# One attention weight in four transfers of 128 rows, in place of one with four rows per partition

## The chip, the core and the metric

The kernel runs on one core of one Trainium2 chip. A core has a matrix engine (PE, with its weight loads shown as PEld), a vector engine (DVE), a scalar engine (ACT), GpSimd (POOL), and a sequencer that here issues nearly all transfers (SP). Sixteen DMA engines move data between the chip's main memory and the core's on-chip memory, which has 128 partitions. The metric is the device time of one execution in microseconds (us); the time of a kernel is the median of its runs.

## What is computed

One token of a decoder block in bfloat16: a layer norm without gain, attention of 32 query heads over a cache of 8 key/value heads with 65,536 positions of 128 numbers each, and a gated layer behind it, both with a residual.

```python
def _A_ref(x, k_cache, v_cache, wq, wo):            # x: 1 x 1 x 512, wq: 512 x 4096
    q = (x @ wq).reshape(B, Sq, Hq, Dh) ...
    scores = jnp.einsum("bhqd,bhkd->bhqk", q, k) * (Dh ** -0.5)
    p = _softmax(scores, axis=-1)
    o = jnp.einsum("bhqk,bhkd->bhqd", p, v)
    return o... @ wo
h = x + _A_ref(_layernorm(x, axis=-1), A_k_cache, A_v_cache, A_wq, A_wo)
h2 = h + _B_ref(_layernorm(h, axis=-1), B_w_gate, B_w_up, B_w_down)   # sigmoid(g) * u, then w_down
```

The caches K and V are 134 MB each. Beside them the weights are small: `wq` and `wo` have 4 MB each, the three weights of the gated layer 5.5 MB together.

## The kernel before

**A list of operations.** The class `Prog` collects, for each engine, a list of operations in the order in which that engine is to run them. Each has names that it waits for (`deps`) and may have a name itself; `emit` turns the names into semaphore waits. A transfer (`dma`) has a semaphore of its own group. An engine works strictly in the order of its list, so a wait holds up everything behind it on that engine. SP's list is nothing but transfers. The first transfer of SP and the first of ACT are taken out of the lists and put ahead of the start-up barrier of the program (lines 192 to 210), so they are issued at once; all others follow behind that barrier.

**The order of the transfers on SP** (lines 341 to 374): first `wq` (line 341, into the buffer `ktw`); then the K cache of head 0 in four transfers of 4 MB, which wait for nothing (lines 343 to 346, issued by line 339 in `load`); then for heads 1 to 7 K and V in halves of 8 MB, alternately (lines 347 to 351), each waiting until the part of the ring buffer that it overwrites has been read; then the last V, `wo` in two parts, the last V's second half, and the weights of the gated layer (`wg`, `wu`, and `wd` in four parts of 8, 3, 2 and 1 rows per partition, 128 partitions each). All of these go through one queue (q1). ACT issues one transfer, the vector `x` of 1 KB (line 325, queue q10).

**`wq` and `x` at the start.** One transfer brings `wq` as 512 rows of 4096 numbers (8 KB a row); partition p receives rows 4p to 4p+3 one behind the other. The vector x must stand in the same order: `x_col[p, k]` is x[4p + k]. It arrives as 16 rows of 32 (`xs`), is spread over the partitions by a matmul with a selecting matrix (line 423), masked and summed by DVE (lines 424 and 427), and goes through the layer norm: sums on DVE (`ln_stats`, lines 400 and 401), totals by a matmul with ones (line 403), mean and variance on DVE (lines 408 to 412), the power -1/2 on POOL (line 414). Line 432 writes the normed x into `xz`, from `hT` (which holds x in the order of `x_col`), the mean and `rstd`.

**The projection** (`project_q`, line 466, called by the operation in line 485) is 32 matmuls: for each of 8 groups of 512 columns four, one for each of the four rows that a partition holds. The operation waits for `wq` and `xz` before its first matmul. It is listed under line 443, where all matmuls with register addresses are made. ACT copies the result out (line 486), DVE transposes it (line 489), ACT spreads it (line 491) and writes the first head's weights (line 500).

**The main part.** For each block of keys DVE transposes chunks of K from the ring into `ktw` (line 531); `ktw` is the buffer that held `wq`, so the first transpose waits for the end of the projection (line 526). PE multiplies the transposed chunks with q (line 443). When DVE has transposed a set of chunks, a tiny DVE operation (line 534) marks it, and SP issues the transfer that overwrites them. Softmax (lines 562 to 580), the transposition of the probabilities (line 587) and the products with V (line 443 again, `ring,PT_sb`) follow for each head.

**The end** is the gated layer: matmuls with `wg` and `wu` (line 847), the gate (lines 854 to 863), matmuls with `wd` (line 866), the copy of the result (lines 884 and 885) and its store (line 886).

Of the kernel before, what the change touches and what calls it, by code (L numbers as in the profile page):

```python
# [10 lines left out]
ALU = mybir.AluOpType  # L11
# [4 lines left out]
NQ = 32  # L16
DH = 128
# [7 lines left out]
NKT = 8  # L25
# [10 lines left out]
class Prog:  # L36
# [14 lines left out]
    def op(self, eng, fn, deps=(), name=None, to=None, times=1):  # L51
        assert name is None or name not in self.where, name
        self.ops[eng].append(dict(fn=fn, deps=[d for d in deps if d], name=name, dma=None, to=to, times=times, part=self.part.get(eng)))
        if name:
            self.where[name] = (eng, len(self.ops[eng]) - 1)

    def dma(self, eng, fn, sem, deps=(), name=None):
        self.op(eng, fn, deps, name)
        rec = self.dma_sems.setdefault(sem, dict(sem=None, count=0))
        rec["count"] += 16  # L60
        self.ops[eng][-1]["dma"] = (sem, rec["count"])
# [162 lines left out]
def bass_sequential_preLN__gqa_block_cached__glu_gated_glu__decode_kernel(  # L224
# [10 lines left out]
    CH = TC * DH  # L235
# [11 lines left out]
    with ExitStack() as es:  # L247
        def sb(name, shape, dt):
            return es.enter_context(nc.sbuf_tensor(name, shape, dt))

        gsel = sb("gsel", [128, 128], fp32)
        hz = sb("hz", [128, 128], fp32)
        identf = sb("identf", [128, 128], fp32)
        onesf = sb("onesf", [128, 128], fp32)
        lsel = sb("lsel", [128, 128], fp32)
        iota_i = sb("iota_i", [128, 128], i32)
        ident = sb("ident", [128, 128], bf16)
# [7 lines left out]
        ktw = sb("ktw", [128, NKT * CH + WH], bf16)  # L265
# [9 lines left out]
        XR = 16  # L275
        xs = sb("xs", [XR, D // XR], bf16)
# [4 lines left out]
        xz = sb("xz", [128, 4 * 16], bf16)  # L281
        qh = sb("qh", [32, 512], bf16)
        qt = sb("qt", [32, 512], bf16)
        hT = [sb(f"hT{i}", [128, 4], fp32) for i in range(2)]
        sq = sb("sq", [128, 4], fp32)
        st = [sb(f"st{i}", [128, 2], fp32) for i in range(2)]
        mo = [sb(f"mo{i}", [128, 4], fp32) for i in range(2)]
        rstd = [sb(f"rstd{i}", [128, 1], fp32) for i in range(2)]
# [26 lines left out]
        def ps(bank, c0, c1, p0=0, p1=128):  # L315
            return PS[p0:p1, bank * 512 + c0: bank * 512 + c1]
# [5 lines left out]
        op, dma = P.op, P.dma  # L322
# [10 lines left out]
        def load(k, h, q, deps, sem, name, cols=None):  # L333
# [4 lines left out]
            at = (first_chunk(k, h, q) - j0) * CH  # L338
            dma("sp", lambda e: e.dma_start(ring[:, at + a * CH:at + z * CH], rows[:, (a - j0) * CH:(z - j0) * CH]), sem, deps, name)  # L339

        dma("sp", lambda e: e.dma_start(ktw[:, 0:NKT * CH].rearrange("p (k n) -> p k n", k=4),
                                        A_wq.rearrange("(p k) n -> p k n", p=128)), "r0", (), "wq")
        for q in range(2):
            for i in range(2):
                j0 = 16 * q + 8 * i
# [52 lines left out]
        def ln_stats(i, parts, dep, bank, c0):  # L398

            op("dve", lambda e: e.tensor_tensor_reduce(hT[i][:, :], parts[0], parts[1], 1.0, 0.0, ALU.add, ALU.add, st[i][:, 0:1]), [dep], f"hT.{i}")  # L400
            op("dve", lambda e: e.tensor_tensor_reduce(sq[:, :], hT[i][:, :], hT[i][:, :], 1.0, 0.0, ALU.mult, ALU.add, st[i][:, 1:2]),
               [f"hT.{i}"], f"st.{i}")
            op("pe", lambda e: e.matmul(ps(bank, c0, c0 + 2), lhsT=onesf[:, :], rhs=st[i][:, :], start=True, stop=True),
               [f"st.{i}", "onesf"], f"tot.{i}")

        def ln_rstd(i, bank, c0, factor):

            op("dve", lambda e: e.tensor_scalar(mo[i][:, 0:2], ps(bank, c0, c0 + 2), 1.0 / D, None, op0=ALU.mult),
               [f"tot.{i}"], f"mo.{i}")
            op("dve", lambda e: e.tensor_tensor(mo[i][:, 2:3], mo[i][:, 0:1], mo[i][:, 0:1], ALU.mult), [f"mo.{i}"], f"m2.{i}")  # L410
            op("dve", lambda e: e.tensor_tensor(mo[i][:, 3:4], mo[i][:, 1:2], mo[i][:, 2:3], ALU.subtract), [f"m2.{i}"], f"var.{i}")
            op("dve", lambda e: e.tensor_scalar(ve[i][:, :], mo[i][:, 3:4], eps, factor, op0=ALU.add, op1=ALU.mult),
               [f"var.{i}"], f"ve.{i}")
            op("pool", lambda e: e.tensor_tensor(rstd[i][:, :], ve[i][:, :], nhalf[:, :], ALU.pow), [f"ve.{i}", "nhalf"],
               f"rstd.{i}")


        n = 128 // XR
# [9 lines left out]
        op("dve", lambda e: None, ["zf"])  # L428
        ln_stats(0, (x_col[:, :], bass.AP(tensor=zf, offset=0, ap=[[1, 128], [0, 4]])), "xcol", 0, 0)
        ln_rstd(0, 0, 0, 1.0)  # L430
        xz_dst = bass.AP(tensor=xz, offset=8, ap=[[4 * 16, 128], [16, 4]])
        op("dve", lambda e: e.tensor_scalar(xz_dst, hT[0][:, :], mo[0][:, 0:1], rstd[0][:, 0:1], op0=ALU.subtract,
                                            op1=ALU.mult), ["rstd.0", "xz0"], "xz")
        def addr_of(t, elements=0):
            return nc.lookup_mloc(t).addr + 2 * elements

# [45 lines left out]

        op("act", lambda e: e.activation(ps(1, 0, 512, 0, 8), bass.AP(tensor=zcol, offset=0, ap=[[1, 8], [0, 512]]), AF.Copy), ["zcol"], "zq")
        op("act", lambda e: e.activation(ps(5, 0, 512), bass.AP(tensor=zcol, offset=0, ap=[[1, 128], [0, 512]]), AF.Copy), (), "zy")
        op("pe", project_q, ["zq", "zy", "xz", "wq", "identf", "lsel", "onef", "sel", "gsel", "row", "PTz", "qz0"], "q")
        op("act", lambda e: e.activation(  # L486
            bass.AP(tensor=qh, offset=0, ap=[[512, 8], [64, 8], [32, 2], [1, 32]]), psap(1, 0, [[64, 8], [1, 2], [2, 32]], 0, 8), AF.Copy),
           ["q", "qh0"], "qh")
# [307 lines left out]
        for i in range(HKV + 1):  # L796
            loop, last = 0 < i < HKV, i == HKV
            for r in range(NR):
# [26 lines left out]
                if not last and r == 3:  # L825
# [9 lines left out]
                                                   op0=ALU.mult, op1=ALU.add), ["tot.1"], "hc")  # L835
# [6 lines left out]
        for i, (nm, bank) in enumerate((("wg", GB), ("wu", UB))):  # L842
            at = W_AT[nm]
            for kt in range(4):
                for c in range(4):
# [3 lines left out]
                        rhs=ring[:, at + kt * FF + c * FG: at + kt * FF + (c + 1) * FG],  # L849
                        start=(kt == 0), stop=(kt == 3), tile_position=(0, 32 * c)),  # L850
# [66 lines left out]
```

## Time and profile before

| | |
|---|---|
| time, median of 3 runs | 656.33 us (656.27 to 656.4) |
| span of the profiled execution | 655.0 us |
| time above that span | 1.33 us (656.33 - 655.0) |
| mean granted clock of PE | 0.786 |
| busy: PE, DVE, ACT, POOL | 397.5, 350.3, 43.1, 3.7 us |
| moved by the DMA engines | 282.33 MB |

The span goes from the first to the last instruction of one profiled execution. For that execution the record holds the span and not a device time; the difference between the median of the runs and the span, 1.33 us, is taken as what lies around the span, and is the same in all the arithmetic below.

How to read it: the profile's page gives busy time by engine, the span in 40 slices, the DMA queues, the chain of work that ended last, the costliest groups of instructions, and the transfers with their time from issue to landing. In the views by window, each row gives a stretch of the span, the busy time of each engine with the number of its instructions, then PE's granted clock, the busy share of the DMA engines, and the rate in GB/s (packets are counted where they start, so in a short stretch the share can be over 1).

### The profile page before, as it was taken

What the parts mean: (1) busy time and instruction counts of PE and PEld (TensorE: products, weight loads), DVE (VectorE), ACT (ScalarE), POOL (GpSimd) and SP (SyncE); (2) the same over time, 40 slices, a digit from 0 to 9 for tenths busy, and PEclk for the clock granted to TensorE, in tenths of its full rate; (3) what the DMA queues carried; (4) which work ended last, traced back from release to release, by engine and by line L of the source; (5) the groups of instructions that cost most, each with busy time, mean ns of one, the idle gap of its engine ahead of it and who ended that gap; (6) DMA issues with size and microseconds to landing.
All of it is one profiled execution on the core that took longest, in us unless ns stands there. A gap on an engine that the chain in (4) does not pass through costs nothing.

```text
span 655.0 us, 6176 instructions
## 1 busy us (share of the span) xinstructions
PE 397.5 (61%) x2317; PEld 66.7 (10%) x1549; DVE 350.3 (53%) x428; ACT 43.1 (7%) x114; POOL 3.7 (1%) x19
## 2 busy tenths in 40 slices
PE   2778672937548293674828467392845739285466
PEld 1100010110101000010100101010010101001122
DVE  3398853819266290935719184481917548092202
ACT  1100200020000200002000200002000020001101
POOL 1000000000000000000000000000000000000000
PEclk9799695977959687785968769596796958878656
DMA  9999999999999999999999999999999989999998
GB/s 400 432 434 462 424 408 448 448 448 412 420 448 448 432 400 448 448 448 404 428 448 448 436 396 448 448 448 416 416 448 448 448 384 448 448 448 424 417 412 363
DMA packets 6372, 282.33 MB, mean 431 GB/s; under 512 B 738, under 2 KB 868, under 8 KB 1252
## 3 DMA queue, kind: packets, MB, share of 16 engines
q1 hardware_dynamic: 6340, 282.33, 99.7%
q10 hardware_dynamic: 32, 0.00, 0.0%
HBM read 282.33 MB, written 0.00 MB: 431 GB/s over the span
## 4 chain that ended last, share of the span: by engine, by line
DMA 66%; DVE 30%; PE 2%; issue 1%; SPq 0%; PEldq 0%
DMA ring<-in_A_k_cache_dram 58%; DVE ktw L531 30%; DMA ring<-in_B_w_up_dram 4%; DMA ring<-in_A_v_cache_dram 4%; PE PS L443 2%; PE PS L866 0%; PE PS L847 0%; DVE hh L859 0%; DVE hhT L863 0%; SPq L368 0%; SPq L339 0%; DVE y_sb L884 0%; PEldq L171 0%
## 5 line engine op out<-in xcount | busy, mean ns | idle before, releaser
L531 DVE STREAM_TRANSPOSE ktw<-ring 128x1024 f32<-128x1024 f32 x256 | 291.5, 1208 | 165.0 <-DMA ring<-in_A_k_cache_dram 165.0
L443 PE MATMUL PS<-ktw 128*128 128x512 bf16 x1024 | 276.3, 419 | 163.4 <-DVE ktw L531 155.8
L443 PE MATMUL PS<-ring,PT_sb 128*32 x1024 | 85.0, 420 | 55.0 <-issue 46.6
L443 PEld LDWEIGHTS PS<-ktw 128*128 x256 | 26.2, 102 | 401.5 <-issue 234.3
L618 ACT ACTIVATE po_sb<-PS,rl 128x512 bf16<-128x512 f32 x8 | 5.5, 687 | 523.4 <-PE PS L443 523.4
L443 PEld LDWEIGHTS PS<-ring,PT_sb 128*32 x1024 | 20.7, 116 | 117.5 <-issue 116.2
L566 DVE TENSOR_REDUCE gmj<-PS 1x4 f32<-1x128 f32 x8 | 2.2, 278 | 53.5 <-PE PS L564 53.5
L538 DVE TENSOR_REDUCE M_sb<-PS 128x1 f32<-128x512 f32 x32 | 19.9, 683 | 19.3 <-PE PS L443 19.3
L577 ACT ACTIVATE P_sb<-PS,negmax 128x512 bf16<-128x512 f32 x32 | 21.6, 686 | 0.3
L587 DVE STREAM_TRANSPOSE PT_sb<-P_sb 128x512 bf16<-128x512 bf16 x32 | 19.9, 674 | 1.7 <-ACT P_sb L577 1.7
L443 PE MATMUL PS<-ktw,xz 128*8 x32 | 9.6, 476 | 6.1 <-DMA ktw<-in_A_wq_dram 6.1
L634 DVE TENSOR_TENSOR Lw<-O,blk_of 128x896 bf16<-128x896 bf16 (+1 forms) x2 | 1.4, 682 | 15.9 <-ACT O L624 15.9
L489 DVE STREAM_TRANSPOSE qt<-qh 32x512 bf16<-32x512 bf16 x1 | 0.7, 699 | 14.8 <-ACT qh L486 14.8
L571 PE MATMUL PS<-one_f,gmrep 1*128 1x1 f32 x16 | 4.7, 358 | 5.0 <-DVE gmrep L568 5.0
L564 PE MATMUL PS<-identf,gm 128*1 128x128 f32 x16 | 4.5, 380 | 5.1 <-issue 2.9
L643 DVE CAST O<-PS 128x28 bf16<-128x28 f32 (+1 forms) x2 | 0.3, 174 | 12.8 <-PE PS L640 12.8
L577 ACT ACTIVATION_READ_ACCUMULATOR P_sb<-PS,negmax 128x1 f32 x32 | 6.5, 203 | 0.0
L621 PE MATMUL PS<-sel_bf,po_sb 128*128 128x4 bf16 x32 | 2.1, 170 | 6.3 <-ACT po_sb L618 6.3
L504 ACT ACTIVATE PS<-zcol 128x512 f32<-128x512 bf16 x8 | 5.0, 622 | 0.0
L573 ACT ACTIVATE negmax<-PS 128x1 f32<-128x1 f32 x8 | 1.4, 171 | 54.0 <-PE PS L571 54.0
L571 PEld LDWEIGHTS PS<-one_f,gmrep 1*128 1x128 f32 x16 | 4.0, 307 | 8.8 <-DVE gmrep L568 8.8
L592 PE MATMUL PS<-L_sb,lsel 128*128 128x4 f32 x16 | 2.5, 229 | 3.8 <-DVE PT_sb L587 3.8
(90 smaller groups left out, 65.4 us busy)
## 6 DMA issues: line engine op xcount, KB each, us to landing
ring<-in_A_k_cache_dram SPq DMA_DIRECT2D x4, 4096.0 KB, 34.8
ring<-in_A_v_cache_dram SPq DMA_DIRECT2D x1, 5120.0 KB, 30.1
ktw<-in_A_wq_dram SPq DMA_DIRECT2D x1, 4096.0 KB, 12.2
ktw<-in_A_wo_dram SPq DMA_DIRECT2D x1, 3584.0 KB, 18.4
ring<-in_A_v_cache_dram SPq DMA_DIRECT2D x1, 3072.0 KB, 36.9
ring<-in_B_w_gate_dram SPq DMA_DIRECT2D x1, 1792.0 KB, 23.4
ring<-in_B_w_up_dram SPq DMA_DIRECT2D x1, 1792.0 KB, 27.2
ring<-in_B_w_down_dram SPq DMA_DIRECT2D x1, 1024.0 KB, 29.2
```

Of the source, the lines that this page charges most:

```text
L443: return e.add_instruction(mybir.InstMatmult(name=nc.get_next_instruction_name(), engine=mybir.EngineType.PE, ins=[rhs, lhsT], outs=[e.low ...
L504: op("act", lambda e: e.activation(ps(PO, 0, 512), bass.AP(tensor=zcol, offset=0, ap=[[1, 128], [0, 512]]), AF.Copy), ["zcol"] if h == 0 e ...
L531: op("dve", lambda e, d=dst, sr=src: e.transpose(d, sr), deps, f"T{b}.{c}", to="T")
L538: op("dve", lambda e, u=u: e.tensor_reduce(M_sb[:, u % 4:u % 4 + 1], ps(u % NS, 0, 512), AX.X, ALU.max), [f"S{b}.{NC - NR + k}"], f"mx{u}" ...
L564: op("pe", lambda e: e.matmul(ps(MISC, 0, 128, 0, 1), lhsT=gm[:, :], rhs=identf[:, :], start=True, stop=True), [f"gm{h}"], f"gmT{h}", to="Q")
L566: op("dve", lambda e: e.tensor_reduce(gmj[:, :], ps(MISC, 0, 128, 0, 1).rearrange("p (i a c) -> p a i c", a=4, c=NC), AX.XY, ALU.max), [f" ...
L571: op("pe", lambda e: e.matmul(ps(MISC, 128, 129), lhsT=gmrep[0:1, :], rhs=one_f[0:1, 0:1], start=True, stop=True), [f"gmrep{h}"], f"neg{h}")
L577: op("act", lambda e, b=b: e.activation(P_sb[:, (b % 4) * 512:(b % 4 + 1) * 512], ps(b % NS, 0, 512), AF.Exp, bias=negmax[:, k:k + 1], sca ...
L587: op("dve", lambda e, b=b: e.transpose(PT_sb[:, (b % 4) * 512:(b % 4 + 1) * 512], P_sb[:, (b % 4) * 512:(b % 4 + 1) * 512]), [f"E{b}"], f" ...
L592: op("pe", lambda e: e.matmul(ps(MISC, 132, 136), lhsT=lsel[:, :], rhs=L_sb[:, :], start=True, stop=True), [f"PT{NR * h + NR - 1}"], f"l{h ...
L618: op("act", lambda e: e.activation(po_sb[:, :], ps(PO, 0, 512), AF.Copy, scale=rl[:, :]), [f"PV{h}.{NR - 1}", f"rl{h}"], f"po{h}", to="po")
L621: op("pe", lambda e, t=t: e.matmul(ps(OX, 0, 4), lhsT=po_sb[:, t * 128:(t + 1) * 128], rhs=sel_bf[:, 8 * t:8 * t + 8:2], start=(t == 0), s ...
```

## The change

`wq` comes in four transfers. Transfer k brings rows 128k to 128k+127, one row of 8 KB to each partition, into the k-th quarter of the same place. Partition p then holds rows p, 128+p, 256+p and 384+p. Only the first of the four is the first transfer of SP and so stands ahead of the start-up barrier. Each has a semaphore of its own, and the projection waits for all four.

x has to stand in the new order for the projection: `xz` now takes x[128k + p]. Four small matmuls bring the 16 rows of `xs` into this order in a bank of PE's result memory (bank 7, columns 48 to 52), each for 32 partitions; they pick columns of the identity matrix with a step of 4. The layer norm's sums go on as they were, from `x_col` in the old order, and so does the residual.

```diff
-        dma("sp", lambda e: e.dma_start(ktw[:, 0:NKT * CH].rearrange("p (k n) -> p k n", k=4),
-                                        A_wq.rearrange("(p k) n -> p k n", p=128)), "r0", (), "wq")
+        for k in range(4):
+            dma("sp", lambda e, k=k: e.dma_start(ktw[:, k * NQ * DH:(k + 1) * NQ * DH], A_wq[128 * k:128 * k + 128, :]), f"q{k}", (), f"wq{k}")
...
+        for j in range(4):
+            op("pe", lambda e, j=j: e.matmul(ps(7, 48, 52, 32 * j, 32 * j + 32), lhsT=xs[:, :], rhs=ident[0:XR, j:XR:4], start=True, stop=True,
+                                             tile_position=(0, 32 * j)), ["x", "ident"] if j == 0 else (), "xq" if j == 3 else None)
         xz_dst = bass.AP(tensor=xz, offset=8, ap=[[4 * 16, 128], [16, 4]])
-        op("dve", lambda e: e.tensor_scalar(xz_dst, hT[0][:, :], mo[0][:, 0:1], rstd[0][:, 0:1], op0=ALU.subtract,
-                                            op1=ALU.mult), ["rstd.0", "xz0"], "xz")
+        op("dve", lambda e: e.tensor_scalar(xz_dst, ps(7, 48, 52), mo[0][:, 0:1], rstd[0][:, 0:1], op0=ALU.subtract,
+                                            op1=ALU.mult), ["rstd.0", "xz0", "xq"], "xz")
...
-        op("pe", project_q, ["zq", "zy", "xz", "wq", "identf", "lsel", "onef", "sel", "gsel", "row", "PTz", "qz0"], "q")
+        op("pe", project_q, ["zq", "zy", "xz", "wq0", "wq1", "wq2", "wq3", "identf", "lsel", "onef", "sel", "gsel", "row", "PTz", "qz0"], "q")
```

## The prediction

> **What bounds the kernel now.** I read the page first: the 40 slices, the queues, and the chain of work that ended last.
>
> ```profile
> span 655.0 us, 6176 instructions
> ...
> DMA  9999999999999999999999999999999989999998
> ...
> DMA packets 6372, 282.33 MB, mean 431 GB/s; under 512 B 738, under 2 KB 868, under 8 KB 1252
> ...
> q1 hardware_dynamic: 6340, 282.33, 99.7%
> ...
> DMA 66%; DVE 30%; PE 2%; issue 1%; SPq 0%; PEldq 0%
> ```
>
> The DMA engines are busy in every slice, the queue q1 for 99.7% of the span. The chain gives DVE 30%, but that alone doesn't say that DVE holds up a transfer. So I looked at the rate in stretches of 19.3 us, at the beginning, and at the long middle.
>
> ```profile
> 0.00:1.00 1.00, 0.00 (x0) 0.00 (x0) 0.00 (x0) 0.00 (x0) 0.20 (x4) 1.00 0.00 0
> 1.00:2.75 1.75, 0.00 (x0) 0.00 (x0) 1.39 (x5) 1.68 (x2) 1.73 (x11) 1.00 1.13 318
> ...
> 11.40:30.70 19.30, 13.43 (x41) 3.71 (x36) 5.20 (x5) 3.24 (x7) 0.00 (x0) 0.85 1.00 433
> 30.70:50.00 19.30, 14.91 (x61) 1.44 (x15) 18.35 (x18) 0.00 (x0) 0.00 (x0) 0.97 1.01 436
> ...
> 69.30:599.40 530.10, 322.27 (x1840) 48.61 (x1168) 295.72 (x335) 31.43 (x88) 0.00 (x0) 0.78 1.00 435
> ```
>
> The last column is GB/s. From 11.4 us on it is 433 to 436, and 435 over 530 us. The stream of transfers begins at 1.0 us, loses something in its first 1.75 us, and then has one rate to the end. 8 MB (8.389 MB, one half of a head's K or V) take 8.389 / 435 = 19.3 us. Now the chain in order of time, for one round of DVE and transfer:
>
> ```profile
> 84.16 24.75 DMA ring<-in_A_k_cache_dram
> 108.91 0.02 issue
> 108.93 13.67 DVE ktw L531 x13
> ```
>
> This K half is issued at 84.16 and lands 24.75 us later. 19.3 of these are its own bytes; 5.4 are left. The first transfer of the kernel, ahead of which nothing stands in the queue, shows how long a lone transfer's lag is:
>
> ```profile
> ktw<-in_A_wq_dram SPq DMA_DIRECT2D x1, 4096.0 KB, 12.2
> ...
> DMA to landing us min/median/max: 21.0/25.7/30.3
> ...
> L339 SPq DMA_DIRECT2D ring<-in_A_k_cache_dram x2: 327/484/641, 0.9 to 1.3; - x2
> ```
>
> `wq` lands at 12.2. The next two lines are the first two K transfers: issued at 0.93 and 1.3, landed 21.0 and 30.3 us later, at 21.9 and 31.6. So 4 MB land every 9.7 us (9.64 by bytes at 435), and `wq` has 12.2 - 9.7 = 2.5 us beside its bytes. A K half that waits 5.4 us beside its bytes has therefore stood some 2.9 us in the queue behind another transfer: DVE hands out the space early enough. **The bound is the stream**, and DVE's 30% of the chain lies beside it.
>
> **The change, part by part.**
>
> *The stream.* The bytes are the same. What changes is the number of pieces. 738 packets are under 512 B, about 16 for each of the 46 transfers (their completions); 6372 - 738 = 5634 are data: 44 transfers of 128 packets, and 2 of the store. `wq` has 128 packets of 32 KB now, 8 on each of 16 engines, and one completion on each. It will have 512 of 8 KB, 32 on each engine, and four completions. The trace holds a very similar group: `wd`, four transfers over 128 partitions, 32 packets per engine, right behind `wu`.
>
> ```profile
> 621.60 0.43 SPq L368 DMA_DIRECT2D ring<-in_B_w_up_dram  x1
> 622.08 1.85 SPq L373 DMA_DIRECT2D ring<-in_B_w_down_dram  x4
> ...
> ring<-in_B_w_up_dram SPq DMA_DIRECT2D x1, 1792.0 KB, 27.2
> ring<-in_B_w_down_dram SPq DMA_DIRECT2D x1, 1024.0 KB, 29.2
> ...
> ring<-in_B_w_down_dram SPq DMA_DIRECT2D x1, 384.0 KB, 29.7
> ring<-in_B_w_down_dram SPq DMA_DIRECT2D x1, 256.0 KB, 29.9
> ring<-in_B_w_down_dram SPq DMA_DIRECT2D x1, 128.0 KB, 29.7
> ```
>
> `wu` lands at 621.60 + 27.2 = 648.8. The last `wd` is issued at 622.08 + 1.85 - 0.43 = 623.5 and lands 29.7 later, at 653.2. Between them lie 4.4 us; the 1792 KB (1.835 MB) take 4.22 at 435. So 32 packets per engine and four completions cost 0.18 us beside their bytes, with 0.1 for the rounding. The `wq` of before has a quarter of these pieces, 0.05. **Net +0.13 us.** The bounds: 0 (the rounding eats it), and +0.3 from the first part of `wd`, which is just a transfer of 8 KB rows: 622.08 + 29.2 - 648.8 = 2.48 us for 2.41 of bytes, 0.07, and four of these are 0.28.
>
> *The start of the stream.* Between 1.00 and 2.75 the rate is 318, so 1.75 x (1 - 318/435) = 0.47 us are lost there. Smaller first packets could lose less or more. No row shows an 8 KB packet on an empty queue; the bounds are -0.47 (all of it hidden) and +1.4 (three further transfers each lose it once more). I take 0, since the loss stands once, ahead of the first data, and the K transfers behind land 9.7 apart without it.
>
> *The issues.* Only the first quarter is issued at 0.00. The second gets the place that the first K transfer has now, at 0.93.
>
> ```profile
> 0.93 2.14 SPq L339 DMA_DIRECT2D ring<-in_A_k_cache_dram  x4
> ...
> 1.31 30.32 DMA ring<-in_A_k_cache_dram
> ```
>
> From issue to the first data the first transfer needs 1.0 us (0.00 to 1.00), so the second quarter can flow at 1.9. The first quarter's bytes (1.049 MB) last 2.41 us, to 3.4 at the earliest. The cover is 1.5 us; were it gone, each us of delay would be one us of the end. The K transfers are issued three issues later, 3 x 2.14/4 = 1.6 us, at 2.5 in place of 0.93, and are needed when `wq` runs out, past 11 us. Behind them in SP's list stand transfers that wait for DVE marks tens of us later. So nothing: 0, as long as the stream has those nine us of work ahead.
>
> *x, its matmuls and the waits.*
>
> ```profile
> 5.06 0.20 PE L423 MATMUL PS<-xs,xpick 16*128 16x32 bf16 x1 [5.06 <-DMA xs<-in_A_x_dram]
> ...
> 6.31 0.58 PE L403 MATMUL PS<-st,onesf 128*128 128x2 f32 x2 [1.05 <-DVE st L401]
> ...
> 8.35 0.30 DVE L432 TENSOR_SCALAR xz<-hT,mo,rstd 128x4 bf16<-128x4 f32 x1 [0.68 <-POOL rstd L414]
> ...
> 12.95 9.64 PE L443 MATMUL PS<-ktw,xz 128*8 x32 [6.05 <-DMA ktw<-in_A_wq_dram]
> ...
> 24.10 4.57 DVE L531 STREAM_TRANSPOSE ktw<-ring 128x1024 f32<-128x1024 f32 x4
> ...
> 31.65 9.13 DVE L531 STREAM_TRANSPOSE ktw<-ring 128x1024 f32<-128x1024 f32 x8 [2.98 <-DMA ring<-in_A_k_cache_dram]
> ```
>
> Four matmuls of 0.20 us come behind line 403, from 6.89 to 7.7; the DVE operation that reads them waits for POOL until 8.35 anyway. It reads them where the matmuls wrote them and not from `hT`; even double its 0.30 it would end at 9.0. PE then stands idle for `wq` until 12.95: cover 4 us. The three added waits stand on PE ahead of the projection, and only work that needs the projection is queued behind them. If the projection starts 0.13 us later, DVE starts 0.13 later than 24.10; but after four chunks, at 28.67, DVE waits 2.98 us for K. So 0, and with this cover gone, the delay alone would be added.
>
> *The end.* The last matmuls need the last `wd`, so the end moves with the stream.
>
> ```profile
> 648.86 1.69 PE PS L847 x16
> ...
> 651.70 1.79 PE PS L866 x50
> ...
> 653.51 0.28 DVE y_sb L884
> ```
>
> **Sum**: the span of 655.0 grows by 0.13 to 655.13; with the 1.33 us that lie between the span and the median of the runs this is 656.46, said as **656.5**.
>
> **The rivals.**
>
> *Slower: every transfer pays its own lag.* If the queue did not run the four quarters into each other, each of the three added transfers would lay open the 2.5 us that `wq` has beside its bytes now: 3 x 2.5 = 7.5, and 656.33 + 7.5 = 663.8. It decides from 1.3 / 3 = 0.44 us per boundary on. Against it: the first K transfers land 9.7 us apart, 0.06 more than their bytes, and the four `wd` together lose 0.18. For it: no such boundary is as early as 1 to 12 us, with the queue just begun. Chance 0.07.
>
> The Trainium skill speaks for this rival in "DMA: Bandwidth & Descriptors", section "Anatomy of one DMA — SWDGE (gpsimd) path": it fits a transfer, issued from GpSimd, as a fixed 2.0 us or so and its bytes at 436 GB/s, which by an estimate for three more would be 6.0 us and 662.3. The same section says that the fixed part is mostly the wait for the receipt of the last write and that the semaphore write costs about a cycle; the landings 9.7 us apart agree with that and not with a sum of fixed parts.
>
> *Slower: the queue runs dry behind the first quarter.* If the second quarter needed as long to its data as x needs to land (`x` shows up on PE at 5.06), it would flow only at some 0.93 + 4.9 = 5.8 and the queue would be empty from 3.4 on: +2.4, 658.7. Against it stands the 1.0 us of the first transfer; x is 1 KB on a queue of its own that shares the engines with 32 KB packets. Chance 0.03.
>
> *A better start and end.* The lag of 0.47 is hidden by smaller packets; and the last matmuls meet a higher clock:
>
> ```profile
> 648.70:651.20 2.50, 2.34 (x18) 0.88 (x18) 1.04 (x3) 0.24 (x1) 0.00 (x0) 0.50 0.99 414
> ```
>
> PE is granted 0.50 there (the number ahead of 0.99). But the last `wd` lands at 653.2 and the last matmuls end at 653.49, so no clock can bring more than 0.29. Both together give 656.33 - 0.76 = 655.6, still within 0.2%. Chance 0.05. For faster by more I see no source: before 1.0 us nothing flows, after it the stream never rests. I leave 0.03 for what I don't see.
>
> *The change does nothing to the stream*: the 32 KB rows were moved in pieces all along. The count of packets above speaks against it; the time would be 656.3. Chance 0.02.
>
> **How the numbers follow.** The forecast has 0.80. A measurement of this kernel can tell about 0.2%, 1.3 us, from no change. Within that lie the forecast, the better start and end, and no effect: 0.87. Slower are the two rivals, 0.10; faster 0.03. The range goes from 655.9 (the start's lag hidden, 656.33 - 0.47) to 657.4 (the forecast with the stream's upper 0.3 and half of the start's 1.4, and a little over); most of the two slower rivals lies outside.
>
> **What would show it.** In the profile after: 6372 + 384 + 48 = some 6800 packets, 48 more under 512 B; the last quarter of `wq` lands at 12.3 or 12.4; the first K transfers land 9.7 us apart, each 0.1 to 0.2 later; DVE still waits nearly 3 us for K before its fifth chunk; 435 GB/s over the middle. Wrong it would be if the quarters landed more than 2.6 us apart, if the rate in the first 4 us showed a hole, or if the end moved by something other than the last landing.

## The result, and the profile after

| | before | changed |
|---|---|---|
| median of the runs | 656.44 us (8 runs, 656.14 to 656.72) | 658.53 us (8 runs, 657.84 to 658.84) |
| span of the profiled execution | 655.0 us | 655.5 us |
| a run less its own span, median | 1.34 us (runs of before beside the later experiments) | 3.46 us (2.84 to 3.68) |

The ratio is 1.0028, with a 95% interval from 1.0019 to 1.0037: slower by 0.28%, 1.8 us (the medians lie 2.1 us apart). Forecast was 656.5, within a range from 655.9 to 657.4. The spans recorded with the eight timed runs of the changed kernel are 654.8 to 655.5 us, five of them 655.0 or 655.1: inside the span nearly nothing has happened. The time was lost around it: each of these runs took 2.84 to 3.68 us more than its own span (the profiled one 658.84 us), and the 2.1 us between 1.34 and 3.46 are all that the medians differ by.

The page of the changed kernel (span, packets by size, the queues):

```profile
span 655.5 us, 6189 instructions
...
DMA packets 6805, 282.35 MB, mean 431 GB/s; under 512 B 786, under 2 KB 916, under 8 KB 1300
...
q1 hardware_dynamic: 6772, 282.33, 99.6%
q8 instruction: 1, 0.02, 0.0%
q10 hardware_dynamic: 32, 0.00, 0.0%
```

48 packets more are under 512 B, as forecast, and 6372 + 384 + 48 = 6804. The page has one more than that, in a line that the page of before lacks: queue q8, kind "instruction", one packet of 0.02 MB. That is not data but code. (Smaller packets of this kind, 8 KB at most, lie on another queue, q14, nearly all in the 11 to 12 us ahead of the span, in every trace and in that of before as well; new is the one on q8.) The transfers of the changed kernel by window show when it came; the row of GB/s has 40 slices of 0.175 us from 653 to 660:

```profile
GB/s 100 35 6 0 0 0 0 0 0 0 0 0 6 94 0 0 0 0 0 0 0 0 0 0 0 0 0 0 0 0 0 0 0 0 0 0 0 0 0 0
...
q1 hardware_dynamic: 36, 0.03, 1.1%
q8 instruction: 1, 0.02, 0.8%
```

The 94 in the fourteenth slice is 94 x 0.175 = 16.4 KB, starting at 655.3 to 655.4. The 6 in the slice before it is the store of the result, issued at 654.35. So a piece of code of 16 KB is read after the result has been sent off, at the end of the span, and on one DMA engine it takes some 0.9 us (0.8% of 16 engines over 7 us).

The start, which the prediction was about: the rate by window, the landings of the quarters (issued at 0.0 the first, at 0.9 and 1.3, then at 1.3 and 1.8), and DVE at its fifth chunk.

```profile
1.00:2.75 1.75, 0.00 (x0) 0.00 (x0) 1.39 (x5) 1.68 (x2) 1.73 (x11) 1.00 0.91 286
...
69.30:599.40 530.10, 320.73 (x1840) 48.11 (x1168) 295.63 (x335) 31.39 (x88) 0.00 (x0) 0.78 1.00 435
```

```profile
L342 SPq DMA_DIRECT2D ktw<-in_A_wq_dram x1: 397/397/397, 0.0 to 0.0; - x1
...
DMA to landing us min/median/max: 4.7/4.7/4.7
...
DMA to landing us min/median/max: 6.4/7.4/8.5
...
DMA to landing us min/median/max: 8.5/9.4/10.4
```

```profile
12.84 8.60 PE L446 MATMUL PS<-ktw,xz 128*8 x32 [6.22 <-DMA ktw<-in_A_wq_dram]
...
31.62 1.25 DVE L534 STREAM_TRANSPOSE ktw<-ring 128x1024 f32<-128x1024 f32 x1 [4.11 <-DMA ring<-in_A_k_cache_dram]
```

The quarters land at 4.7, 7.3, 9.8 and 12.2, about 2.5 us apart; the last of them when the one transfer landed before. DVE gets its fifth K chunk at 31.62 (31.65 before) and has waited 4.11 us for it. The middle still flows at 435.

### The profile page after: what moved, and what is told of

Its sections match the earlier page's. It is cut to its first block, busy times and chain, and to the rows that moved or that the text cites. A ratio compares the mean times of both kernels' runs of the same rounds, so it can differ in the third digit from the quotient of the medians.

```text
span 655.5 us, 6189 instructions
## 1 busy us (share of the span) xinstructions
PE 396.1 (60%) x2321; PEld 65.8 (10%) x1553; DVE 350.2 (53%) x428; ACT 43.1 (7%) x114; POOL 3.7 (1%) x19
## 4 chain that ended last, share of the span: by engine, by line
DMA 66%; DVE 30%; PE 2%; issue 1%; SPq 1%; PEldq 0%
DMA ring<-in_A_k_cache_dram 58%; DVE ktw L534 30%; DMA ring<-in_B_w_down_dram 5%; DMA ring<-in_A_v_cache_dram 4%; PE PS L446 2%; SPq L342 0%; SPq L373 0%; SPq L368 0%; PE PS L869 0%; SPq L339 0%; DVE y_sb L887 0%; PEldq L171 0%
```

## The experiments

**Theory L**, from that line of the page: PE's list of instructions, longer by four matmuls (a weight load and a matmul each) and one wait, passes an edge between two pieces of code, and the piece behind the edge is fetched late. **Rival S**: the four transfers, or their three more semaphores, cost the time somewhere outside the span. **Rival M**, against the next results: each small matmul costs a share by what it does.

**Four transfers in the old order of rows**, no matmuls added:

```diff
+        for k in range(4):
+            dma("sp", lambda e, k=k: e.dma_start(ktw[:, k * NQ * DH:(k + 1) * NQ * DH], A_wq.rearrange("(p k) n -> p k n", k=4)[:, k, :]), f"q{k}", (), f"wq{k}")
```

> wq in four transfers with a semaphore each, but in the old order of rows (partition p still holds rows 4p to 4p+3, transfer k brings row 4p+k), so x and the matmuls of before stay. The profiled span of the changed kernel is only 0 to 0.5 us longer than before while the time of a run is 2.1 us longer, and its trace shows a 16 KB packet of kind instruction at the very end. Theory L (the list of PE instructions has grown past an edge in its code, and a piece of code is fetched late): this kernel adds one wait to PE's code and no matmul, so no instruction packet, and 656.4 to 656.6 (ratio 1.000 to 1.0005). Rival S (the four transfers cost the time, in the stream or by three more semaphores): 658.5, ratio 1.003.

Measured: 656.39 us, ratio 1.0002 (0.9993 to 1.0011), span 655.0. All that is new in the stream is here (6804 packets, four semaphores), and it costs nothing that can be measured. Rival S falls.

**One transfer, but in the new order, with the four matmuls:**

```diff
+        dma("sp", lambda e: e.dma_start(ktw[:, 0:NKT * CH].rearrange("p (k n) -> p k n", k=4),
+                                        A_wq.rearrange("(k p) n -> p k n", p=128)), "r0", (), "wq")
```

> wq in one transfer as before, but with its rows in the new order (512 packets of 8 KB), and x arranged to match with the four small matmuls. PE's code has the four matmuls more, and no added wait. Theory L: 658.5, ratio 1.003, with a packet of kind instruction in the trace, span within 0.5 us of before. Rival S: 656.4 to 656.6.

Measured: 660.20 us, ratio 1.0056 (1.0042 to 1.0070), with the packet of code. Slower, as L says, and by more than the whole change. The five runs differ: the profiled one took 658.05 us, the other four 660.1 to 660.3.

**The kernel before with four unread matmuls:**

```diff
+        for j in range(4):
+            op("pe", lambda e, j=j: e.matmul(ps(7, 48, 52, 32 * j, 32 * j + 32), lhsT=xs[:, :], rhs=ident[0:XR, j:XR:4], start=True, stop=True,
+                                             tile_position=(0, 32 * j)), ["x", "ident"] if j == 0 else ())
```

> The kernel before, wq and x as they were, with the four small matmuls added behind the layer norm's; nothing reads what they write. Theory L: 658.5, ratio 1.003, with a packet of kind instruction at the end. Rival S: as before, 656.4, ratio 1.000, no such packet.

Measured: 660.27 us, ratio 1.0056 (1.0042 to 1.0070); the size was 3.9 us where 2.1 was expected. The span is 655.0 as before, so all of it lies outside. The transfers of this run from 653 to 660, in slices of 0.175 us as above:

```profile
DMA  0000000000000000000500000000000000000000
GB/s 0 0 0 0 0 0 0 0 0 6 0 0 0 0 0 0 0 0 0 94 0 0 0 0 0 0 0 0 0 0 0 0 0 0 0 0 0 0 0 0
...
q8 instruction: 1, 0.02, 1.3%
q1 hardware_dynamic: 4, 0.00, 0.1%
```

The store is in the tenth slice, at 654.6 to 654.75; the read of the code starts at 656.3 to 656.5, behind the end of the span.

**The changed kernel with four matmuls less elsewhere**, at the end of PE's code (one row of the last part of the `wo` projection left out, so the output lacks it):

```diff
-        project(range(NQ - GS, NQ), O3, ["O3.1", "wo1"], last=True)
+        project(range(NQ - GS + 1, NQ), O3, ["O3.1", "wo1"], last=True)
```

> The changed kernel with four matmuls less elsewhere: one row of the last head group's part of the wo projection is left out (rows 29 to 31 in place of 28 to 31, four matmuls of line 653), so PE's code is about as long as before (one wait more) and the output lacks that part. These matmuls lie 3 us ahead of the landing that the end waits for. Theory L: 656.4 to 656.6, ratio 1.000 to 1.0005, no packet of kind instruction. Rival S: 658.5, ratio 1.003.

Measured: 656.45 us, ratio 1.0000 (0.9991 to 1.0009), span 655.0. The same four matmuls at the start, the same transfers, and no packet of code; the same window:

```profile
GB/s 0 0 0 0 0 0 0 0 0 6 0 0 0 0 0 0 0 0 0 0 0 0 0 0 0 0 0 0 0 0 0 0 0 0 0 0 0 0 0 0
...
DMA packets 4, 0.00 MB, mean 0 GB/s; under 512 B 2, under 2 KB 4, under 8 KB 4
```

What the added matmuls do costs nothing; that PE's code has grown does. But do a few instructions more cost a share each?

**One, two and eight unread matmuls** in the place of the four:

> The kernel before with one unread small matmul (a weight load and a matmul, two instructions of PE's code) in the place of the four. Theory L (an edge in PE's code, which one wait more does not reach and four matmuls do): either 656.4, ratio 1.000 and no packet of kind instruction, or 658 to 660.5 with one; nothing between. Rival M (each of the small matmuls costs its share, (660.3 - 656.4) / 4 = 1.0 us, by what it does): 657.4, ratio 1.0015.

Measured: 656.86 us, ratio 1.0005 (0.9996 to 1.0014), no packet of code.

> The kernel before with two unread small matmuls, four instructions of PE's code. Theory L: 656.4 or 658 to 660.5, and a packet of kind instruction with the second only. Rival M: 658.3, ratio 1.003.

Measured: 660.07 us, ratio 1.0054 (1.0040 to 1.0067), with the packet. The same window has it in the slice that starts at 657.2:

```profile
GB/s 0 0 0 0 0 0 0 0 0 6 0 0 0 0 0 0 0 0 0 0 0 0 0 0 94 0 0 0 0 0 0 0 0 0 0 0 0 0 0 0
...
q8 instruction: 1, 0.02, 0.8%
```

> The kernel before with eight unread small matmuls, sixteen instructions of PE's code. Theory L: 658 to 660.5 as with four, one packet of kind instruction: the edge is passed once. Rival M: 656.4 + 8 x 1.0 = 664, ratio 1.012.

Measured: 657.65 us, ratio 1.0020 (1.0011 to 1.0029): eight cost less than two. Rival M falls. One packet of code was expected at the end; it came, but in the middle. Here the window from 95 to 105 us, and the chain of this kernel over the same stretch:

```profile
q1 hardware_dynamic: 63, 4.13, 96.2%
q8 instruction: 1, 0.02, 0.6%
```

```profile
83.95 26.36 DMA ring<-in_A_k_cache_dram
110.33 9.13 DVE ktw L534 x8
```

This K half lands at 110.31, 1.4 us later than the 108.91 of before, and `wu`, the last big transfer, at 650.06 in place of 648.82. The end of the span moves as much: 656.3, and the median is 1.35 us above it, as before. So the same 16 KB, read while the stream runs, hold up nothing at the end but cost time in the stream: 0.6% of 16 engines over 10 us is 0.96 us on one engine, somewhat less than the 1.24 us by which `wu` is late; the rest is not explained. How a read on one engine moves the end shows in the last transfers, here of this kernel in the window from 653 to 660:

```profile
GB/s 29 23 23 23 23 23 12 0 0 0 0 0 0 0 0 0 6 0 0 0 0 0 0 0 0 0 0 0 0 0 0 0 0 0 0 0 0 0 0 0
```

For 1.2 us (seven slices of 0.175) only some 23 GB/s flow, where the stream of before is over at 653. A sixteenth of the 435 GB/s is 27. That fits one engine that still has packets when the other fifteen have none: in the 550 us since the read it has not caught up.

**The whole change without its matmuls**, x brought into the new order by a second transfer of ACT:

```diff
+        dma("act", lambda e: e.dma_start(xo[:, :], A_x[0].rearrange("o (k p) -> (o p) k", p=128), allow_slow_non_contiguous=True), "xo", name="xo")
```

> The whole change without its four matmuls: wq in four transfers of 128 rows, and x brought into the new order by a second small transfer of ACT (512 pieces of 2 bytes) in place of the matmuls. PE's code has one wait more than before. Theory L: no packet of kind instruction, 656.4 to 656.7 (the small pieces may take 0.3 us of the stream), ratio 1.000 to 1.0005. Rival M: 656.4 too. If the order of x or the four transfers cost the time: 658.5, ratio 1.003.

Measured: 660.66 us, ratio 1.0058 (1.0044 to 1.0072): the expectation failed, but by another way. The span is 659.7, so this loss lies inside. The chain begins with that transfer:

```profile
0.93 20.85 DMA xo<-in_A_x_dram
...
22.68 9.90 PE PS L445 x32
...
34.09 16.03 DVE ktw L533 x15
```

512 pieces of 2 bytes take 20.85 us beside the big packets. The projection starts at 22.68 in place of 12.95, DVE at 34.09 in place of 24.10; ten us are more than the cover of 3 us that DVE has ahead of its fifth chunk, and the space for the next K half is handed out late (at 52.2 in place of 45.3). The run has no packet of code, and the profiled execution took 661.03 us, 1.3 above its span, as in the kernel before. That agrees with L, but the time itself says nothing on L here.

**The whole change with a shorter PE part**: x comes a second time as 4 rows of 128, one matmul brings it into the new order, the four transfers share a semaphore.

```diff
+        dma("act", lambda e: e.dma_start(x4[:, :], A_x[0].rearrange("o (k p) -> (o k) p", p=128)), "x4", name="x4")
...
-            dma("sp", lambda e, k=k: e.dma_start(ktw[:, k * NQ * DH:(k + 1) * NQ * DH], A_wq[128 * k:128 * k + 128, :]), f"q{k}", (), f"wq{k}")
+            dma("sp", lambda e, k=k: e.dma_start(ktw[:, k * NQ * DH:(k + 1) * NQ * DH], A_wq[128 * k:128 * k + 128, :]), "q", (), f"wq{k}")
...
+        op("pe", lambda e: e.matmul(ps(7, 48, 52), lhsT=x4[:, :], rhs=ident[0:4, 0:4], start=True, stop=True), ["x4", "ident"], "xq")
```

> The whole change with a shorter PE part: x comes a second time, as 4 rows of 128 in a small transfer of ACT, so one matmul brings it into the new order in place of four, and the four transfers of wq share one semaphore, so PE has one wait on them. PE's code has two instructions more than before, as with the one unread matmul. Theory L: no packet of kind instruction near the end, 656.3 to 656.9, ratio 1.000 to 1.0007. If the four transfers or the new order cost time by themselves: 658.5, ratio 1.003.

Measured: 656.66 us, ratio 1.0002 (0.9993 to 1.0011), span 655.1, no packet of code. The change as such costs nothing that can be measured, and gains nothing.

**The changed kernel, made longer still**, by four more small matmuls:

```diff
+        for j in range(4):
+            op("pe", lambda e, j=j: e.matmul(ps(7, 48, 52, 32 * j, 32 * j + 32), lhsT=xs[:, :], rhs=ident[0:XR, j:XR:4], start=True, stop=True,
+                                             tile_position=(0, 32 * j)), ["x", "ident"] if j == 0 else ())
```

> The changed kernel with four more small matmuls, whose results are overwritten by the four that count: PE's code is 17 instructions longer than before in place of 9. Theory L, as the run with eight unread matmuls shows it: the code is now fetched in the middle of the kernel, near 100 us, and not at the end; the fetch costs about 1.2 us of the stream there and nothing behind the end, so 657.4 to 657.8, ratio 1.002, faster than the changed kernel by 0.9 though it has more to do. If each added instruction costs (rival M): 658.5 + 4 x 1.0 = 662, ratio 1.009.

Measured: 657.75 us, ratio 1.0019 (1.0010 to 1.0028), span 656.4; the packet of code is in the middle again, between 95 and 106 us:

```profile
q1 hardware_dynamic: 66, 4.33, 91.0%
q8 instruction: 1, 0.02, 0.5%
```

It is not slower than the changed kernel, with four matmuls more. Whether it is really faster stays open: the two intervals overlap.

**The kernel before, made shorter** by the same row of the `wo` projection:

> The kernel before with one row of the last head group's part of the wo projection left out (four matmuls less at the end of PE's code, the output lacks that part). It tells whether the kernel before pays something of that kind too. Theory L: no packet of kind instruction in before, so nothing to gain: 656.3 to 656.5, ratio 0.9995 to 1.0005. If shorter PE code is faster in general: 655.5 or less, ratio under 0.999.

Measured: 656.55 us, ratio 1.0005 (0.9995 to 1.0014). Before has nothing of that kind to lose.

Put together, by how many instructions PE's code is longer than before:

| instructions of PE more | runs | code read | time above before |
|---|---|---|---|
| -8, +1, +1, +2, +2 | shorter before, old order, trimmed change, one matmul (two kernels) | no packet on q8 | 0.0 to 0.4 us |
| +4, +8, +8, +9 | two matmuls, one transfer, four unread, the change | 654.8 to 657.2 us, at the end | 2.1 to 3.9 us |
| +16, +17 | eight unread, longer change | near 100 us, in the stream | 1.2 and 1.3 us |

A small matmul is two instructions (the profile of before has 6176, that with four unread matmuls 6184); the three added waits of the projection make PE's list longer by one. The third column has the start of the slice in which the read starts, in the one execution of each kernel that has a trace. The last column is the median less that of before in the same set of runs. The kernel with the second transfer of x in 512 pieces is left out.

## Why the prediction was wrong

**The stream: nothing speaks against the mechanism, and the term is too small to be told.** Forecast were +0.13 us, bounds 0 and 0.3. The run with the four transfers alone gives 1.0002 (0.9993 to 1.0011), that is -0.5 to +0.7 us. In the profile of the change the last quarter lands at 12.2 as before (12.3 or 12.4 was forecast), and the first K transfers at 21.9 and 31.6, no later than before (0.1 to 0.2 later was forecast). The packets are those that were counted. The start's loss was put at no change: 1.75 x (1 - 286/435) = 0.60 us after, 0.47 before. The queue did not run dry, and no transfer laid open a lag of its own: the quarters land 2.5 us apart.

**x, its matmuls and the waits: right in what was priced.** The operation that reads them starts at POOL's end as before, and DVE had more cover at its fifth chunk than forecast: 4.11 us in place of nearly 3, because the 32 matmuls of the projection took 8.60 us in place of 9.64 and DVE began the sooner. Why they were shorter is not shown; nothing hangs on it, since DVE waits for K in both kernels.

**The step that failed is the sum**, in the term that was carried over unchanged: "with the 1.33 us that lie between the span and the median of the runs". It took what lies around the span as constant, and the four matmuls were priced by their time on PE alone, "So 0". They also have a place in PE's code. With four to nine instructions more, 16 KB of code are read when the result is already on its way, and the time above the span goes from 1.34 us to 3.46 in the changed kernel. So the sign of being wrong that did appear is the last that the prediction names, a time that moves by something other than the last landing. The chance left for slower, 0.10, was all on the two rivals of the stream, and neither of them happened.

What is shown: the cost goes with the length of PE's code and with the packet of code, in the change and in the ten other kernels of the table; it is not the transfers, nor the order of rows, nor what the matmuls do. SP's list alone, with three transfers more, does not bring it. Nor does the number of instructions of all engines together: by the pages the kernel with two unread matmuls has 6180 and pays, the one with four transfers in the old order also has 6180, the trimmed change 6181, the one with one matmul 6183, and these don't. Whether a longer list on another engine has such a price was not tried. What is inferred: that the end of the execution waits for this code. The record of instructions ends with the span and does not show the wait itself. Of the 16 KB the Trainium skill speaks in "Runtime: NRT & Kernel Launch", section "Instruction fetch mechanics": each engine's instructions are read in blocks of 16 KiB through a DMA queue of its own, and a crossing is called mostly hidden. The size agrees (16.4 KB by the slice); that it is hidden does not fit the times here, neither at the end (2.1 to 3.9 us) nor in the stream (1.2 us).

Open stays why the late read costs 2.1 us in the changed kernel and 3.6 to 3.9 in the kernels with four or eight instructions more. In the four executions with a trace the read starts at 654.8 (one transfer in the new order), 655.3 (the change), 656.3 (four unread matmuls) and 657.2 (two), and they took 658.05, 658.84, 660.34 and 659.61 us. In the first three a later read goes with a longer time; the fourth does not fit. The code alone doesn't set the cost either: the kernel with one transfer took 658.05 us in this execution and 660.1 to 660.3 in the others, whose reads are not on record. Open is also why sixteen instructions more move the read from the end to near 100 us. The 0.4 us with one unread matmul are within its interval.

## What to carry to other kernels

A change can have a price in code beside its price in work. Compare each run with its own span, before and after, since a loss around the span is seen in no chain and no busy time; and look for packets of kind "instruction" in a window of the transfers that reaches beyond the end of the span. The page is not enough for that, since it ends with the span: in the kernels with four and with two unread matmuls it lacks the line of q8, because the reads start at 656.3 and 657.2 and the spans are 655.0 and 655.1 us. If a small change costs more than any of its operations can, add unread instructions to the old kernel, and take as many away elsewhere in the new one. Where a kernel sits just below such an edge, pay for new instructions by shortening the same engine's list, as the trimmed change and the one with one matmul do here.

## What the runs showed of the hardware

- A block of code is one packet of 16 KB, 0.9 to 1.4 us long in these records. When it falls into a stream that is the bound, the whole kernel ends about 1.2 us later: with eight unread matmuls the K half behind it landed 1.4 us late, `wu`, 540 us further on, still 1.24 us, and the last 1.2 us of the stream flow at 23 GB/s, about one engine's share.
- Longer code was cheaper: with eight unread matmuls 657.65 us, with two 660.07.
- 512 pieces of 2 bytes beside 8 KB and 32 KB packets took 20.85 us from issue to landing; x as 16 rows of 64 bytes took 3.6 in the same kernel.
